# Attention forward and backward with constant matmuls ahead of the gradient bursts, the backward stream two half-steps later, value tiles double buffered, and the normalisation in two parts

## The chip, the cores and the metric

The kernel runs on one core of a Trainium2 chip. The metric is the device time of one execution in microseconds (us), the median over several. The core has five engines that run side by side: TensorE (PE in the profile; its weight loads are listed apart, as PEld), VectorE (DVE), ScalarE (ACT), GpSimd (POOL) and SyncE (SP), whose queue issues nearly all DMAs here. [...]

## The reference

The program computes a layer and its gradients. The layer mixes an attention block and a state-space convolution with a gate. Only the attention part matters for the change:

```python
B, S, D, H = 1, 2048, 576, 32          # Dh = D // H = 18
def _A_ref(x, wqkv, wo):
    qkv = (x @ wqkv).reshape(B, S, 3, H, Dh).transpose(2, 0, 3, 1, 4)
    q, k, v = qkv[0], qkv[1], qkv[2]
    scores = jnp.einsum("bhqd,bhkd->bhqk", q, k) * (Dh ** -0.5)
    p = softmax(scores, axis=-1)
    o = jnp.einsum("bhqk,bhkd->bhqd", p, v)
    return o.transpose(0, 2, 1, 3).reshape(B, S, D) @ wo
...
g = sigmoid((x * gate_w).sum(-1, keepdims=True))
return g * a + (1 - g) * b             # a: attention, b: the convolution
```

The kernel returns this output and the gradients of all twelve differentiated inputs for a given `grad_out`. For attention that means dQ, dK and dV, with P recomputed where it is needed: dV = P^T dO, dP = dO V^T, dS = P * (dP - rowsum(dO * O)), dQ = dS K, dK = dS^T Q.

## The kernel before

The program has stages one after the other: projections and preparation, attention (forward and backward), a stage that forms the weight gradients of attention, the convolution with its gradients, and the sum. The change touches attention alone.

**Tiles.** 32 heads of width 18 are padded to 32 partitions, so four heads fill 128. A head group `g` (8 of them) has transposed tiles `QaT`, `KaT`, `VaT` (128 x 2048) and token-major tiles `Vtok`, `Ktok`, `Qtok`, loaded in `load_group` (L364 on). `QaT`, `KaT` and `Vtok` have two buffers, `VaT`, `Ktok` and `Qtok` one. A unit is a group and one of four blocks of 512 queries: 32 units.

**Two streams in one loop.** The loop over `G` counts half-steps, 32 per unit (`NST`), 1024 in all. In each, the forward stream of one unit computes two score tiles P1 (keys on partitions; two of the four heads), and the backward stream of an earlier unit, `OFF = NST + 5 = 37` half-steps behind (`G2 = G - OFF`), computes two score tiles P3 (queries on partitions) and two tiles P2 = V dO^T. These are the rows: six matmuls of 32 x 128 weights on 512 columns, in two sets of three (x = 0, 1). Each set works on three different 32-row strips of PE, so its three run side by side. P1 and P3 go to PSUM tag `S` (four buffers), P2 to `dP` (two).

**After the rows come the bursts, then ACT and DVE.** The order on PE, ACT, DVE and POOL is the program's own (`manual_schedule`); SP's order is set by the framework. In each half-step, PE runs the rows and then one or two bursts of 128-row, 32-column matmuls, four of which work side by side on the four column strips:

- `G % 4 == 1`: `dv_burst`, 8 matmuls of 512 columns (`accV`), eight tiles `eb` times `dOa`;
- `G % 4 == 2`: `dq_burst`, 8 of 512 columns (`accQ`), two tiles `ds` times `Ktok`;
- `G % 4 == 3` and `0`: half of dK each, 8 of 256 columns (`accK`, from the transposed `dsT`), and after it `accO`, 4 of 512 columns, the forward P V of one key tile.

All three gradient accumulators share one PSUM buffer, `accB`. ACT then takes exp of the P1 tiles (`PT`, L593) and the P3 tiles (`eb`, L597), four in all; DVE multiplies the two P2 tiles by P (`ds`, L602) and then adds the burst's accumulator to its sum in SBUF (`dvacc` L462, `dqa` L479, `dkacc` L503). When a `ds` tile is complete, SP issues its transpose `dsT` (L608).

**At the end of a unit's forward** `post_forward` makes three steps. f0 (ACT) copies `accO` to `oT`. f1, two half-steps later and ahead of that half-step's rows, transposes it on PE into a tile of tag `S` (`ps_o`), and on DVE divides by the row sum (`rl`, `Ob`), scales dO (`dOa`), and forms the row sums of dO * O (`prod`, `dl`, into `dOa`); then SP stores `Ob` to `O_d` (L409). f2, at the same place, has SP transpose `dOa` to `dOaT` (L413), which the backward stream's P2 reads. `dOa` has three buffers by hand.

**Gradients leave** through `store_grad`: an ACT copy `gb` (L419), a DMA transpose `gT` (L421), a POOL copy `dtk` (L423) and a store (L424); once per unit for dQ, eight times per group for dV and dK.

Every matmul is issued by the helper in L30, so the profile shows that line for all of them; they are told apart by their tiles. In `out<-in,in` the streamed operand stands first and the weights second: `ps_P<-QaT_g,KaT_g` is P1, `ps_P<-KaT_g,QaT_g` P3, `ps_P<-dOaT,VaT_g` P2.

## Time and profile before

| | us |
|---|---|
| median of 4 executions | 3944.19 (3938.09 to 3949.21) |
| the profiled execution | 3926.11 |
| its span | 3924.4 |
| first P1 row to last accK result (attention) | 243.1 to 2525.9 |
| PE idle for VaT_g, 392 to 2350 us | 33.0 (7 times) |
| DVE `ds` (L602) idle for PE, same stretch | 202.6 |
| mean granted TensorE clock, whole span | 0.64 of full speed |

The page gives, for each engine, its busy time, and then the span in 40 slices of 98 us, with a digit for the busy share in tenths. The line `PEclk` is the share of full speed that the chip grants TensorE in that slice. Matmuls are pipelined and their ends are modelled, so a PE that reads as busy need not be at its peak rate. A group line has the program line, engine, operation, tiles, shapes and count, then busy time and mean duration of one, then the engine's idle time just before, and what ended it.

### The profile page before, as it was taken

The page shows a single profiled execution, that of the slowest core. Times are in us where ns is not written, and L with a number is a line of the kernel's source. Part 1 is how long each engine was busy: PE and PEld are TensorE (multiplying, and loading weights), DVE is VectorE, ACT ScalarE, POOL GpSimd, SP SyncE. Part 2 cuts the span into 40 slices and gives each one's busy share as a digit, 9 for nine tenths or more (in the row PEclk, how much of TensorE's full clock was granted, in tenths as well). Part 3 has the DMA queues.
Part 4 walks back from the last instruction along what each step waited for, and adds up shares of the span by engine and source line. Part 5 has one row for each costly group of instructions (what it writes and reads, how often), then busy time and mean ns, then how long its engine had stood idle before and what let it go on. Part 6 is the DMA issues. An engine that isn't in the chain of part 4 may idle for free. (4 is left out here: it accounts for less than half of the span.)

```text
span 3924.4 us, 64060 instructions
## 1 busy us (share of the span) xinstructions
PE 3017.0 (77%) x24020; PEld 1067.3 (27%) x24020; DVE 2945.2 (75%) x5131; ACT 2842.0 (72%) x5253; POOL 63.2 (2%) x147
## 2 busy tenths in 40 slices
PE   7979999999999999999999999679344554445421
PEld 2312222222222222222222222145133333333320
DVE  5618878878878878878878878625288888888867
ACT  4559999999999999999989999410266666666610
POOL 0000000000000000000000000100000000000000
PEclk9956666656665656665666667589555555555555
DMA  8535686775686785686776686875455666555456
GB/s 196 170 93 131 135 159 135 137 162 129 134 162 130 136 162 131 138 160 132 143 159 131 138 152 128 193 207 148 71 97 108 110 110 113 104 101 103 85 146 194
DMA packets 1860137, 536.78 MB, mean 137 GB/s; under 512 B 1774991, under 2 KB 1838553, under 8 KB 1859826
## 3 DMA queue, kind: packets, MB, share of 16 engines
q1 hardware_dynamic: 1859826, 532.69, 64.9%
q8 instruction: 189, 3.10, 0.3%
q14 instruction: 122, 1.00, 0.1%
HBM read 99.74 MB, written 60.96 MB: 41 GB/s over the span
## 5 line engine op out<-in xcount | busy, mean ns | idle before, releaser
L602 DVE TENSOR_TENSOR ds<-ps_P,PT 128x512 bf16<-128x512 f32 x2048 | 1359.4, 687 | 351.0 <-PE ps_P L30 225.6
L593 ACT ACTIVATE PT<-ps_P 128x512 bf16<-128x512 f32 x2048 | 1316.1, 647 | 135.9 <-PE ps_P L30 127.1
L597 ACT ACTIVATE eb<-ps_P 128x512 bf16<-128x512 f32 x2048 | 1333.2, 653 | 20.9 <-PE ps_P L30 20.8
L30 PE MATMUL ps_P<-dOaT,VaT_g 32*128 32x512 bf16 x2048 | 1045.6, 537 | 45.6 <-DMA VaT_g<-VaT_d 33.0
L30 PE MATMUL ps_P<-KaT_g,QaT_g 32*128 32x512 bf16 x2048 | 1007.1, 528 | 37.7 <-ACT PT L593 3.2
L30 PE MATMUL ps_P<-QaT_g,KaT_g 32*128 32x512 bf16 x2048 | 960.7, 543 | 34.4 <-DMA KaT_g<-KaT_d 6.0
L30 PEld LDWEIGHTS <-KaT_g 32*128 32x128 bf16 x2048 | 148.5, 101 | 656.6 <-issue 641.6
L30 PEld LDWEIGHTS <-VaT_g 32*128 32x128 bf16 x2048 | 191.8, 96 | 412.9 <-issue 368.2
L30 PE MATMUL accO<-PT,Vtok_g 128*32 128x512 bf16 x2048 | 301.8, 573 | 0.0
L30 PE MATMUL accK<-dsT,Qtok_g 128*32 128x256 bf16 x4096 | 287.5, 374 | 5.5 <-DVE dqa L479 3.5
L30 PE MATMUL accQ<-ds,Ktok_g 128*32 128x512 bf16 x2048 | 238.4, 558 | 1.4 <-DVE dvacc L462 0.8
L30 PE MATMUL accV<-eb,dOa 128*32 128x512 bf16 x2048 | 233.3, 547 | 0.6 <-DVE dkacc L503 0.6
L30 PEld LDWEIGHTS <-QaT_g 32*128 32x128 bf16 x2048 | 172.0, 97 | 187.3 <-issue 175.9
L30 PE MATMUL uvp<-RX,E1e 128*128 128x64 bf16 x1152 | 134.2, 290 | 106.8 <-DVE E1e L901 106.8
L30 PE MATMUL tps<-RX,T0w 128*128 128x32 bf16 x576 | 38.4, 233 | 215.0 <-DVE yd L1036 202.6
L882 ACT ACTIVATE kk<-ph,magc 128x512 f32<-128x512 f32 x144 | 91.0, 685 | 147.5 <-DVE E1e L900 112.7
L30 PE MATMUL ph<-thr,lrow 3*128 3x512 bf16 x288 | 126.2, 567 | 88.0 <-ACT ab L875 60.2
L462 DVE TENSOR_TENSOR dvacc<-dvacc,accV 128x512 f32<-128x512 f32 x224 | 153.3, 684 | 28.8 <-PE accV L30 25.4
L479 DVE TENSOR_TENSOR dqa<-dqa,accQ 128x512 f32<-128x512 f32 x224 | 153.1, 684 | 24.8 <-PE accQ L30 20.5
L30 PEld LDWEIGHTS <-E1e 128*128 128x128 bf16 x1152 | 125.3, 124 | 127.8 <-DVE E1e L901 127.2
L30 PE MATMUL ybp<-Rw,E1n 128*128 128x31 bf16 x1152 | 70.2, 233 | 103.7 <-ACT ydi L973 101.0
L887 DVE SCALAR_TENSOR_TENSOR kk<-kk,ph 128x512 f32<-128x512 f32 x144 | 95.1, 682 | 71.8 <-ACT kk L882 71.7
(267 smaller groups left out, 3329.3 us busy)
## 6 DMA issues: line engine op xcount, KB each, us to landing
T0w<-Kp_d SPq DMA_DIRECT2D x36, 512.0 KB
dsT<-ds SPq DMA_TRANSPOSE x512
dqkv_d<-dtk SPq DMA_DIRECT2D x96, 72.0 KB
dqkv_tok<-dqkv_d SPq DMA_DIRECT2D x1, 6912.0 KB
Md_d<-mst SPq DMA_DIRECT2D x144, 36.0 KB
ga_d<-ga_st SPq DMA_DIRECT2D x16, 288.0 KB
dxm_d<-dxm SPq DMA_DIRECT2D x16, 288.0 KB
skw<-Md_d SPq DMA_DIRECT2D x72, 64.0 KB
```

Of the source, the lines that this page charges most:

```text
L30: return nc.tensor.matmul(out, lhsT=lhsT, rhs=rhs, start=start, stop=stop, **kw)
L462: nc.vector.tensor_tensor(a_, a_, acc, op=A.add)
L479: nc.vector.tensor_tensor(U["dqa"], U["dqa"], acc, op=A.add)
L593: nc.scalar.activation(U["PT"][i][:, j, :], ps, ACT.Exp)
L597: nc.scalar.activation(e, ps, ACT.Exp)
L602: nc.vector.tensor_tensor(U["ds"][i][:, j, :], ps, U["PT"][i][:, j, :], op=A.mult)
L882: nc.scalar.activation(B_["kk"][h][:, 4 * q:4 * q + 4, :], ph, ACT.Identity, bias=magc, scale=1.0)
L887: nc.vector.scalar_tensor_tensor(v_, v_, MAGIC, B_["ph"].pop((h, q)), op0=A.subtract, op1=A.subtract)
```

## The change

Seven things change, all inside the attention stage:

- `fill` issues matmuls of a constant (`J_bf`, a reversed identity, as weights; `ident_bf`, read four times over, as 512 streamed columns) over the whole 128 x 128 array, into the accumulator that the next burst will overwrite. There is one ahead of the dV burst, one ahead of dQ, three ahead of the first half of dK (`NFILL = (1, 1, 3)`).
- `OFF` is `NST + 7` in place of `NST + 5`. The bursts now go by `G2 % 4` and stay at their places within the backward stream; `accO` stays at `G % 4 == 3` and `0` and is now issued ahead of the fill and the burst. So per four half-steps: `accO`, fill, `accV` | `accO`, fill, `accQ` | three fills, `accK` | `accK`.
- `VaT` has two buffers in place of one.
- f1 keeps the transposes, `rl`, `Ob` and `dOa`. f2 takes `prod`, `dl`, the last write to `dOa`, the store to `O_d` and the transpose `dOaT`, and runs one half-step after f1.
- `PT` has 21 buffers in place of 20, `eb` 10 in place of 12, `dOa` two in place of three.
- `oT`, `rl`, `Ob`, `dl` and `dqa` have one buffer in place of two.
- The accumulator of a burst is taken ahead of it and handed over by a list, `ACC`.

```diff
+            NFILL = (1, 1, 3)
...
-                ptp = ctx.enter_context(tc.tile_pool(name="ptp", bufs=20))
+                ptp = ctx.enter_context(tc.tile_pool(name="ptp", bufs=21))
...
-                for u in range(3):
+                for u in range(2):
...
-                    for nm, src, nb in (("QaT", QaT_d[g], 2), ("KaT", KaT_d[g], 2), ("VaT", VaT_d[g], 1)):
+                    for nm, src, nb in (("QaT", QaT_d[g], 2), ("KaT", KaT_d[g], 2), ("VaT", VaT_d[g], 2)):
...
+                        st["Ob"] = Ob
                         nc.vector.tensor_tensor(Ob, po[:, :, :, 0:DH], rlb, op=A.mult)
                         nc.vector.tensor_tensor(da[:, :, :, 0:DH], U["dO"], rlb, op=A.mult)
+
+                    def f2():
+                        da, Ob = U["dOa"], st["Ob"]
                         prod = work.tile([P, TPQ, 4, DH], F32, tag="prod", bufs=1, name="prod")
                         nc.vector.tensor_tensor(prod, da[:, :, :, 0:DH], Ob, op=A.mult)
...
                         nc.sync.dma_start(O_d[:, b * TPQ:(b + 1) * TPQ, 4 * g * DH:4 * (g + 1) * DH], Ob.rearrange("p t a b -> p t (a b)"))
-
-                    def f2():
                         U["dOaT"] = work.tile([P, TPQ, P], BF, tag="dOaT", name="dOaT")
...
-                OFF = NST + 5
+                OFF = NST + 7
...
+                ACC = []
+                fill_r = ident_bf.unsqueeze(1).to_broadcast([P, 4, P])
+
+                def fill(acc, n, w=4):
+                    o_ = acc[:, (4 - w) * P:4 * P].rearrange("p (a b) -> p a b", b=P)
+                    for _ in range(n):
+                        mm(o_, lhsT=J_bf, rhs=fill_r[:, 0:w, :])
+
                 def dv_burst(g, b, kq, half):
                     U = UN[(g, b)]
-                    acc = accB("accV")
+                    acc = ACC.pop()
...
+                    ph = G2 % 4 if 4 <= G2 < NTOT + 4 + (0, 1, 6, 0)[G2 % 4] else None
+                    if ph == 2 and G2 < 10:
+                        ph = None
...
-                                at(("pre", G + 2), f2)
+                                at(("pre", G + 3), f2)
+                    if ph in (0, 1, 2):
+                        ACC.append(accB(("accV", "accQ", "accK")[ph]))
+                        fill(ACC[0], NFILL[ph])
+                    if G2 % 4 == 0 and G2 >= 4:
...
+                            evs.append(dv_burst(g, b, q_ // 2, q_ % 2))
...
+                    if G2 % 4 == 1 and G2 >= 5:
...
+                            evs.append(dq_burst(g, b, q_))
...
+                    if G2 % 4 in (2, 3) and G2 >= 10:
...
+                            e_ = dk_half(g, b, q_, h_, dkst)
...
-                            e = work.tile([P, KB], BF, tag="eb", bufs=12, name="eb")
+                            e = work.tile([P, KB], BF, tag="eb", bufs=10, name="eb")
```

## The prediction

> **What bounds the kernel now.** I read the page first, then the groups of the attention stretch, then its timeline and clock. From the page:

> ```profile
> PE 3017.0 (77%) x24020; PEld 1067.3 (27%) x24020; DVE 2945.2 (75%) x5131; ACT 2842.0 (72%) x5253; POOL 63.2 (2%) x147
> ...
> PE   7979999999999999999999999679344554445421
> ...
> ACT  4559999999999999999989999410266666666610
> ...
> PEclk9956666656665656665666667589555555555555
> ```

> Slices 4 to 25 are the attention part. PE and ACT both read 9, and the TensorE clock is granted at only 0.5 to 0.7. The groups of 392 to 2350 us, by line, operation, shapes and count, busy time, mean ns, idle before:

> ```profile
> L602 DVE TENSOR_TENSOR ds<-ps_P,PT 128x512 bf16<-128x512 f32 x1774 | 1177.7, 687 | 317.2 <-PE ps_P L30 202.6 <-issue 43.9 <-ACT eb L597 41.7
> L597 ACT ACTIVATE eb<-ps_P 128x512 bf16<-128x512 f32 x1774 | 1159.8, 654 | 0.0
> L593 ACT ACTIVATE PT<-ps_P 128x512 bf16<-128x512 f32 x1773 | 1146.4, 647 | 124.2 <-PE ps_P L30 115.5
> L30 PE MATMUL ps_P<-dOaT,VaT_g 32*128 32x512 bf16 x1773 | 912.8, 538 | 40.8 <-DMA VaT_g<-VaT_d 33.0 <-DVE ds L602 5.5 <-DMA dOaT<-dOa 2.0
> ```

> DVE and ACT wait for PE, and PE waits 33.0 us (7 times) for the value tile of a new head group. Then the timeline of one half-step at full clock (start, duration, engine, line, operation):

> ```profile
> 1509.08 0.39 PE L30 MATMUL ps_P<-QaT_g,KaT_g 32*128 32x512 bf16 x1
> ...
> 1510.18 0.38 PE L30 MATMUL ps_P<-dOaT,VaT_g 32*128 32x512 bf16 x1
> 1510.49 0.40 PE L30 MATMUL accK<-dsT,Qtok_g 128*32 128x256 bf16 x8
> 1510.72 0.39 PE L30 MATMUL accO<-PT,Vtok_g 128*32 128x512 bf16 x4
> 1511.04 0.38 PE L30 MATMUL ps_P<-QaT_g,KaT_g 32*128 32x512 bf16 x1
> ```

> From one first row to the next 1.96 us pass. In that time ACT runs four exponentials, whose ends lie 0.49 apart (1511.59, 1512.07, 1512.57), so 4 x 0.49 = 1.96: at full clock ACT is the bound. Measured over the whole stretch (starts of the first P1 row of each half-step, 985 of them with both streams, 284.7 to 2451.5 us) the mean is 2.198. Half-steps 14 to 31 of a unit, away from the unit change, average 2.098; of these the ones wholly at half clock 2.155, wholly at full clock 1.971. Last, the clock in windows (busy us of PE, weight load, DVE, ACT, POOL; then the clock):

> ```profile
> 1504.00:1507.41 3.41, 3.41 (x29) 0.71 (x27) 2.81 (x5) 3.17 (x7) 0.00 (x0) 0.50 0.49 102
> 1507.41:1510.83 3.42, 3.08 (x36) 1.03 (x32) 3.33 (x7) 3.42 (x8) 0.00 (x0) 1.00 0.42 96
> 1510.83:1514.24 3.41, 2.97 (x32) 0.99 (x24) 2.83 (x5) 3.41 (x9) 0.00 (x0) 1.00 0.65 147
> 1514.24:1517.65 3.41, 3.41 (x27) 0.64 (x26) 2.58 (x5) 3.27 (x8) 0.00 (x0) 0.50 0.68 154
> ```

> The clock changes only at steps of 3.41 us. What decides it is not PE's busy time but the share of the array in use. I counted, per window, the columns streamed times the share of the array that the shape occupies (a 32x512 row: 128; the eight of accV or accQ: 1024; eight of accK: 512; four of accO: 512). Of 460 half-clock windows 85 were followed by full clock; their count has a 10th percentile of 2908 and a median of 3072, while 90% of the others lie under 2950. Of 172 full-clock windows 84 were followed by half clock, all with a count under 3190; of the 88 that stayed, 11 lie below 3072. So about 3072 per window is the mark. Four half-steps now hold 24 rows, accV, accQ, 2 accK, 2 accO = 7168; at 7.84 us that is 3120 per window, just at the mark, and full clock is lost after two windows as a rule (27% of windows).

> **The change, part by part.** *Fill.* Five matmuls of 512 columns on the whole array per four half-steps add 2560: 9728 per period. Their price. A 512-column step takes 0.22 us at full and 0.42 at half clock (eight accQ took 0.61 and 1.04, one 0.39 and 0.62). Going from rows to a burst takes 0.31 from start to start at full clock, so 0.09 beside the step, and 0.53 at half; from burst to rows 0.31 and 0.56. Switching to and from a whole-array matmul inside a burst has no row; it lies between 0 (accK to accO, same shape, no gap) and 0.14 (burst to rows at half clock), and I take 0.09. The bursts also move: accO now precedes accV (one half-step) and accQ (the next), then accK alone with three fills, then accK alone. What these read (PT, eb, ds, dsT) is older than the rows ahead of them, so the order adds no wait.

> At full clock, accO + fill + accV: rows to accO 0.31, to fill 0.31, to accV 0.31, second group 0.22, to the next rows 0.31 = 1.46. From the fourth exponential's end to its row 0.06, row 0.39, exponential 0.60: 0.06 + 1.46 + 0.39 + 0.60 = 2.51, where ACT wants 1.96 + 0.49 = 2.45. So two of four half-steps are 0.06 late: 2.02. With accK and three fills 0.31 + 0.44 + 0.31 + 0.11 + 0.21 = 1.38, on time: 1.96, as is the last. Period 7.96, mean 1.99. At half clock 0.41 (first to second rows) + 0.53 + 0.56 + 0.53 + 0.42 + 0.56 = 3.01 for the three filled ones, about 2.1 for the fourth (today's accK median): mean 2.78.

> The count per full window is then 9728 x 3.41 / 7.96 = 4170 on average. But a window over the unfilled half-step holds 16 rows' worth (its own and the next, 1536), one accK (512) and some 0.4 us of burst: about 2880. Sliding a window over this timeline, 11% of positions lie under 3072. The window after such a one starts at a filled burst, dense enough to come back (2816 per 3.01 us = 3190 per window). So I take nine full windows to one half: 30.7 / 1.99 + 3.41 / 3.01 = 16.56 half-steps in 34.1 us = 2.06. Gain (2.098 - 2.06) x 985 = 37 us.

> *Value tiles double buffered.* The load leaves the group change; 33.0 us of PE idle go, up to 34.5 by the seven long half-steps (7.26 mean against 2.33 for others there). Next late there would be Ktok and Qtok, still single: PE's loads wait 2.4 us for Qtok now. Gain 31, bounds 0 to 34.

> *Normalisation in two parts.* Half-steps 1 to 4 of a unit cost 0.91 + 0.38 + 0.57 - 0.24 = 1.6 us over 2.098. Its DVE chain (0.26 + 0.46 + 0.45 + 0.46 + 0.45 + 0.20 = 2.28) stood in one piece ahead of two products of 0.69; now 1.17 and 1.11 in successive half-steps. The second part carries the O_d store and the dOaT transpose to the next half-step on SP's queue, where dsT transposes follow them; with the backward stream two later, dOaT has four half-steps instead of three. The transposes on PE and the wait for rl and Ob before ps_o's buffer comes free remain. I take 0.5 of the 1.6, x 31 units = 16, bounds 0 and 50.

> *Copies on ACT.* With ACT the bound, oT, one gb of dqa and on average two of dvacc and dkacc per unit cost 4 x 0.49 = 1.96; 0.55 of it shows already (half-step 10), about 0.9 falls into the 0.06 gaps. Loss 0.5 x 31 = 16, bounds 0 and 40.

> *Two half-steps later.* Two more with P1 alone (1.12) and with the gradients alone (2.0), two fewer of 2.2: loss 2. Fewer buffers for eb, dOa, dqa, oT: each is read out a half-step or more before its reuse (eb's burst ends some 0.8 us ahead), so nothing; were that cover gone, one wait of that order per period.

> Sum: -37 - 31 - 16 + 16 + 2 = -66. The profiled execution took 3926.1 (span 3924.4), so 3860; it lies 18 under the median 3944.19, so the median becomes **3878**.

> [...]

> **The rivals.**

> *Full clock throughout.* If the count never falls under the mark, the mean is 1.99: (1.99 - 2.098) x 985 = -106, sum -135, **3809**. For it: the average is a third above the mark. Against: the unfilled half-step.

> *Half clock too often (slower).* At half clock a filled half-step costs 3.01 against 2.155 before. The point from which this decides is where the full-clock share of time falls under 0.77: there 1 / (0.77/1.99 + 0.23/2.78) = 2.13, which eats the other terms (-29 / 985 = -0.03). At 0.65 the mean is 2.21: +110 - 29, **4025**. For it: the low window comes round every eight or nine, and the stall at each unit change can drop the clock once more, and a half-clock window over the unfilled half-step holds about 1280 + 1.3/3.0 x 2816 = 2500, below the mark. Against: three dense half-steps in a row.

> *A wait takes the place.* All bursts share one accB buffer, and a fill writes it, so it waits for DVE's evacuation earlier than the burst did; rows and exponentials queue behind it. accQ's last result comes 0.31 x 3 + 0.22 + 0.39 = 1.54 after the rows, the evacuation ends at 2.23, the next fill is due at 2.33: 0.1 to spare, with DVE at 2 x 0.66 + 0.69 = 2.01 of 2.02. Were two fills per period 0.13 late, 246 x 0.26 = 64 would be lost: **3942**, no change.

> *The fill does not count.* If constant operands do not move the clock, its share stays 0.27: 1 / (0.27/1.99 + 0.73/2.78) = 2.51, +406 - 29: **4321**. Nothing in the trace of before shows a matmul on such data.

> **How the numbers follow.** Chances: forecast 0.47, full clock 0.17, the wait 0.13 (0.04 faster, 0.07 same, 0.02 slower), half clock 0.20, not counted 0.03. About 0.2%, 8 us, is what a measurement of this kernel can tell. So faster 0.68, same 0.07, slower 0.25. The forecast's own range is 3836 to 3936: the unseen switch at 0 gives 30 less, at 0.2 some 50 more, and the bounds of the split and copies add to it. The range from full clock to most of the half-clock case is 3805 to 4000; about 0.07 lies below and 0.12 above.

> **What would show it.** Granted clock of 0.9 or more in slices 5 to 24, PE's wait for VaT_g gone, half-steps of 2.02, 2.02, 1.96, 1.96 in full windows and about 3.0 in half ones, the 317 us that ds waits for PE smaller. A clock near 0.8 with PE at 9 means the second rival; idle of PE before the fill, released by dqa or dvacc, the third; 0.6 the fourth. The prediction is wrong if the full-clock share leaves 0.8 to 1, or if the switch to the whole array costs far from 0.09.

## The result, and the profile after

| | before | after |
|---|---|---|
| median, us | 3941.86 (48 runs) | 3950.68 (29 runs) |
| ratio to before | | 1.0027, 95% interval [1.0019, 1.0036] |
| span of the profiled execution, us | 3924.4 | 3950.0 |
| half-step with both streams, mean, us | 2.198 (986 of them) | 2.210 (984) |
| mean granted TensorE clock, 600 to 2300 us | 0.63 | 0.91 |

The change makes the kernel 0.27% slower, where 1.7% faster was forecast. The clock rose, though not quite as far as foreseen (nine full windows to one half would be a mean of 0.95), and the half-steps did not get shorter. The page of the changed kernel, the lines that answer to those of before:

```profile
PE 3031.7 (77%) x25300; PEld 1099.4 (28%) x25300; DVE 2906.2 (74%) x5131; ACT 2841.6 (72%) x5253; POOL 63.0 (2%) x146
...
PE   7979999999989999999999999768345544445421
...
ACT  4549999989989989999989999500266666666610
...
PEclk9958999988989989989989989888655555555555
```

PE has 1280 more matmuls (the fills), the clock line reads 8 or 9 through the attention slices instead of 5 to 7, and ACT falls from 9 to 8 in every third slice or so. The groups of 392 to 2350 us (busy time, mean ns, idle before):

```profile
L619 DVE TENSOR_TENSOR ds<-ps_P,PT 128x512 bf16<-128x512 f32 x1765 | 1153.6, 685 | 180.9 <-PE ps_P L30 179.6 <-issue 0.2
L614 ACT ACTIVATE eb<-ps_P 128x512 bf16<-128x512 f32 x1766 | 1116.6, 632 | 0.0
L610 ACT ACTIVATE PT<-ps_P 128x512 bf16<-128x512 f32 x1765 | 1104.6, 626 | 129.6 <-PE ps_P L30 124.0
L30 PE MATMUL ps_P<-dOaT,VaT_g 32*128 32x512 bf16 x1764 | 698.9, 414 | 1.5 <-DMA dOaT<-dOa 0.7 <-DVE ds L619 0.4
L30 PE MATMUL accK<-ident_bf,J_bf 128*128 128x512 bf16 x663 | 188.8, 395 | 19.1 <-DVE dqa L490 14.3 <-DVE dqa L488 3.4
```

A row now takes 0.41 us on average where it took 0.54, and the wait for VaT_g (33.0 us) is gone. But in the same 1958 us the kernel gets through 1765 tiles where it got through 1774. ACT sits idle for 129.6 us before `PT` (124.0 of them for PE), much as before (124.2, 115.5 for PE). The clock in windows of 3.41 us shows the main reason (window, length, busy us of PE, weight load, DVE, ACT, POOL; then clock, DMA share, GB/s):

```profile
1235.06:1238.47 3.41, 3.41 (x24) 0.72 (x27) 2.16 (x4) 3.19 (x8) 0.04 (x1) 0.50 0.87 168
1238.47:1241.88 3.41, 3.08 (x37) 0.90 (x31) 2.36 (x4) 2.99 (x7) 0.39 (x1) 1.00 0.80 151
1241.88:1245.30 3.42, 3.20 (x31) 0.82 (x24) 2.64 (x6) 3.42 (x8) 0.00 (x0) 1.00 0.61 114
1245.30:1248.71 3.41, 3.41 (x36) 1.01 (x31) 3.34 (x6) 3.38 (x8) 0.00 (x0) 1.00 0.53 100
1248.71:1252.12 3.41, 3.19 (x33) 0.88 (x25) 2.67 (x6) 3.41 (x8) 0.00 (x0) 1.00 0.78 136
1252.12:1255.54 3.42, 3.42 (x24) 0.57 (x20) 2.27 (x4) 2.52 (x6) 0.00 (x0) 0.50 0.75 142
...
1269.19:1272.60 3.41, 3.41 (x24) 0.59 (x20) 2.18 (x4) 2.44 (x6) 0.00 (x0) 0.50 0.80 152
```

In this stretch every fifth window is at half clock, and in it ACT is idle for 0.2 to 1 us. The window ahead of the second one, 1248.71 to 1252.12, on PE:

```profile
1249.79 0.40 PE L30 MATMUL accK<-dsT,Qtok_g 128*32 128x256 bf16 x8
1250.12 0.39 PE L30 MATMUL ps_P<-QaT_g,KaT_g 32*128 32x512 bf16 x1
...
1251.46 0.39 PE L30 MATMUL ps_P<-dOaT,VaT_g 32*128 32x512 bf16 x1
1251.77 0.40 PE L30 MATMUL accO<-PT,Vtok_g 128*32 128x512 bf16 x4
1252.10 0.61 PE L30 MATMUL accV<-ident_bf,J_bf 128*128 128x512 bf16 x1
1252.64 1.04 PE L30 MATMUL accV<-eb,dOa 128*32 128x512 bf16 x8
```

It is the window over the half-step without a fill: but for the tail of the burst before, the accK half at 1249.79 is its only gradient burst, and the next fill starts as it ends. Counted as in the prediction it holds 2850 columns, under the mark of about 3072 that the trace of before gave. Of 78 such drops from 300 to 2400 us, 48 come after a window that begins in the half-step with three fills, mostly late in it, and 26 after one that begins in the half-step with none; 30 of them lie exactly five windows after the one before, 10 lie ten windows after. 62 of the drops last one window, the other 16 two to eight.

### The profile page after: what moved, and what is told of

It reads as the page before. It is cut to its first block, busy times and chain, and to the rows that moved or that the text cites. A ratio compares the mean times of both kernels' runs of the same rounds, so it can differ in the third digit from the quotient of the medians.

```text
span 3950.0 us, 66344 instructions
## 1 busy us (share of the span) xinstructions
PE 3031.7 (77%) x25300; PEld 1099.4 (28%) x25300; DVE 2906.2 (74%) x5131; ACT 2841.6 (72%) x5253; POOL 63.0 (2%) x146
## 5 line engine op out<-in xcount | busy, mean ns | idle before, releaser
L610 ACT ACTIVATE PT<-ps_P 128x512 bf16<-128x512 f32 x2048 | 1270.8, 625 | 142.1 <-PE ps_P L30 135.8
L614 ACT ACTIVATE eb<-ps_P 128x512 bf16<-128x512 f32 x2048 | 1285.7, 630 | 24.7 <-PE ps_P L30 24.6
L30 PE MATMUL ps_P<-dOaT,VaT_g 32*128 32x512 bf16 x2048 | 807.2, 413 | 5.1 <-DVE ds L619 3.5
L30 PE MATMUL ps_P<-KaT_g,QaT_g 32*128 32x512 bf16 x2048 | 736.8, 406 | 45.2 <-ACT PT L610 11.1
L30 PE MATMUL ps_P<-QaT_g,KaT_g 32*128 32x512 bf16 x2048 | 724.3, 415 | 44.2 <-ACT PT L610 13.1
L30 PEld LDWEIGHTS <-VaT_g 32*128 32x128 bf16 x2048 | 174.9, 92 | 375.4 <-issue 370.6
L30 PEld LDWEIGHTS <-KaT_g 32*128 32x128 bf16 x2048 | 138.1, 94 | 398.7 <-issue 395.2
L30 PE MATMUL accK<-ident_bf,J_bf 128*128 128x512 bf16 x768 | 217.8, 394 | 24.6 <-DVE dqa L490 18.2
L30 PE MATMUL accO<-PT,Vtok_g 128*32 128x512 bf16 x2048 | 235.3, 444 | 0.0
L30 PEld LDWEIGHTS <-J_bf 128*128 128x128 bf16 x1344 | 120.5, 99 | 363.0 <-issue 294.8
L30 PE MATMUL accK<-dsT,Qtok_g 128*32 128x256 bf16 x4096 | 211.1, 284 | 6.8 <-DMA Qtok_g<-QaT_d 6.7
L30 PE MATMUL uvp<-RX,E1e 128*128 128x64 bf16 x1152 | 134.2, 290 | 106.6 <-DVE E1e L918 106.6
L30 PE MATMUL tps<-RX,T0w 128*128 128x32 bf16 x576 | 38.4, 233 | 215.0 <-DVE yd L1053 190.9
L30 PE MATMUL ph<-thr,lrow 3*128 3x512 bf16 x288 | 128.0, 580 | 86.9 <-ACT ab L892 59.3
L30 PE MATMUL accV<-eb,dOa 128*32 128x512 bf16 x2048 | 191.2, 457 | 0.0
L30 PEld LDWEIGHTS <-QaT_g 32*128 32x128 bf16 x2048 | 153.1, 92 | 135.4 <-issue 132.0
L30 PE MATMUL accQ<-ds,Ktok_g 128*32 128x512 bf16 x2048 | 171.6, 415 | 4.8 <-DMA Ktok_g<-KaT_d 4.8
L30 PEld LDWEIGHTS <-E1e 128*128 128x128 bf16 x1152 | 125.2, 123 | 127.3 <-DVE E1e L918 126.7
```

The lines of the kernel that those rows point to most:

```text
L30: return nc.tensor.matmul(out, lhsT=lhsT, rhs=rhs, start=start, stop=stop, **kw)
L610: nc.scalar.activation(U["PT"][i][:, j, :], ps, ACT.Exp)
L614: nc.scalar.activation(e, ps, ACT.Exp)
```

## The experiments

Times are medians; ratios are of means, to the kernel before on the same chip (its median there 3936 to 3944), with 95% intervals. "Full period" is the sum, over the four places in a period, of the median half-step that lies wholly at full clock, each from its first P1 row to the next one's. A "drop" is a change from full to half clock; drops and half-clock windows are counted from 300 to 2400 us. Eleven kernels ran.

**Without the fills.**

```diff
-            NFILL = (1, 1, 3)
+            NFILL = (0, 0, 0)
```

> The changed kernel with its five fills per period left out (NFILL 0, 0, 0); all else stays. Theory A (the clock eats the gain: the fills raise the share of full clock, but the one half-step without a fill drops it every fourth or fifth window, and a filled period costs 11.3 us at half clock against 8.0): without fills the granted clock in attention falls from 0.90 to 0.60-0.68, a period at full clock 7.84 us, at half clock 8.8-9.2, and the time is within 25 us of the changed kernel (3930 to 3975). Rival B (the fills cost by themselves, through PE time and the single accB buffer, also at full clock): 40 us or more faster than the changed kernel, below 3910. Rival C (bunching accO with accV and accQ is what costs): still slower than the kernel before, 3960 or more, with dV and dQ half-steps of about 2.4 us at half clock.

3972.6, ratio 1.0076 [1.0059, 1.0093]. The clock of 600 to 2300 us, in the changed kernel and then without fills:

```profile
600.00:2300.00 1700.00, 1609.57 (x13340) 434.13 (x13336) 1329.65 (x2256) 1585.24 (x3166) 30.92 (x72) 0.91 0.80 142
600.00:2300.00 1700.00, 1594.50 (x12242) 401.09 (x12246) 1336.63 (x2231) 1564.76 (x3129) 29.47 (x69) 0.71 0.80 141
```

PE is busy 94% of the time without fills at a clock of 0.71, and 95% in the changed kernel at 0.91: the constant matmuls do move the clock, and busy time does not tell it. They bring 0.5%. That falls on theory A's side and against B as a whole, with the clock a little above A's bound. But C fits as well, by its time and by its half-steps: at half clock the one with accO and accQ takes 2.37 us, the one with accO and accV 3.00.

**Bursts spread again, no fills.** accO goes to the two accK half-steps.

```diff
-                    if G % 4 in (3, 0) and G >= 3:
-                        i_ = (G - 3) // 4 * 2 + (1 if G % 4 == 0 else 0)
+                    if G % 4 in (1, 2) and G >= 2:
+                        i_ = (G - 2) // 4 * 2 + (1 if G % 4 == 1 else 0)
```

> As e1, and accO moved two half-steps, so that it stands with the two accK halves as in the kernel before: the stall edits alone (double-buffered value tiles, split normalisation, stream two later) with bursts spread as before. Theory A: half-steps 16 to 31 of a unit as in the kernel before (2.09 us), granted clock 0.6-0.65, the stalls at the unit change 2 us per unit less: 45 to 70 us faster than the kernel before, 3875 to 3900. Rival (the stall edits bring nothing because something else is late at the unit change): within 15 us of the kernel before.

3920.8, ratio 0.9951 [0.9936, 0.9966]: 19 us faster than before, less than expected, and 1.25% faster than e1. So C is right in part: having accO beside accV and accQ costs 49 us without fills (a period at half clock takes 9.21 us in e1 and 8.65 here). PE's waits show what the stall edits ran into (total, times, longest):

```profile
PEld L30 <- DMA Qtok_g<-QaT_d: 27.8, 7, 5.1
PE accK L30 <- DMA Qtok_g<-QaT_d: 24.9, 7, 4.8
```

The wait for VaT_g at the seven group changes, in half-step 5 of a unit, became one for Qtok_g in half-step 17.

**Bursts spread, with fills.** accO as in e2, with one fill ahead of accV, accQ and the first accK half (`NFILL` 1, 1, 1); then two at the last place (1, 1, 2).

> As e2 with one fill ahead of accV, accQ and the first accK half. Counted on a full-clock timeline of 1.96 us per half-step, the emptiest window holds 3072 columns, and 1% of positions are under the mark. Theory A: granted clock 0.95 or more in attention, half-steps 16 to 31 of 1.97 to 2.0 us, time 3770 to 3830. Rival B (the fill's own cost or the accB wait): full clock, but half-steps of 2.1 or more, time above 3880.

> As e3_bal_fill111 with two fills ahead of the first accK half. Theory A: the same as with one within 15 us, since the emptiest window is the one over the half-step without a fill (3072 columns in both). Rival B: slower by 20 us or more, about 245 x 0.1 to 0.2.

With one: 3867.7, ratio 0.9804 [0.9783, 0.9824], clock 0.94, full period 7.84 us, which is ACT's 16 x 0.49. The period held and the size did not (3770 to 3830 was expected): half-steps 16 to 31 average 2.08, Qtok_g is waited for here too (24.9 us, all in half-step 17), and the clock drops 41 times. Runs of 46 to 60 windows at full clock occur between them. With two: 3903.9, ratio 0.9895 [0.9878, 0.9912], full period 7.98. Here rival B was right: a second fill in that half-step lies on the path, 0.14 us a period.

**Value tile back to one buffer; normalisation back to one part.** Each alone, in the changed kernel.

```diff
-                    for nm, src, nb in (("QaT", QaT_d[g], 2), ("KaT", KaT_d[g], 2), ("VaT", VaT_d[g], 2)):
+                    for nm, src, nb in (("QaT", QaT_d[g], 2), ("KaT", KaT_d[g], 2), ("VaT", VaT_d[g], 1)):
```

> The changed kernel with VaT back in one buffer; all else stays. Theory A (the double buffer took the 33 us wait away, but Qtok and Ktok, still single, are late next and give a part back: 11.5 us in the changed kernel's trace): PE's wait for VaT_g returns with 25 to 35 us, that for Qtok_g and Ktok_g goes to under 4, time 10 to 25 us above the changed kernel, 3960 to 3976. Rival (the next late load takes all of it): within 8 us of the changed kernel.

3966.7, ratio 1.0088 [1.0056, 1.0120]. The wait for VaT_g is back, and that for Qtok_g falls to 2.1:

```profile
PE ps_P L30 <- DMA VaT_g<-VaT_d: 40.0, 7, 6.9
```

The second buffer is worth 0.6%, 24 us (by the intervals some 13 either way), as theory A had it.

```diff
-                        st["Ob"] = Ob
...
-                    def f2():
-                        da, Ob = U["dOa"], st["Ob"]
...
+                    def f2():
                         U["dOaT"] = work.tile([P, TPQ, P], BF, tag="dOaT", name="dOaT")
...
-                                at(("pre", G + 3), f2)
+                                at(("pre", G + 2), f2)
```

> The changed kernel with the normalisation in one part again (prod, dl and the O_d store in f1, the dOaT transpose at the same place); all else stays. The prediction priced the split at 16 us (0 to 50): by it 3960 to 3975. Rival (the wait for ps_o and the ACT copies set the stall at the unit change, not the length of DVE's chain): within 8 us of the changed kernel.

3980.1, ratio 1.0125 [1.0085, 1.0165]: the split is worth about 1.0%, 39 us (some 16 either way), over twice the 16 of the prediction. Half-step 3 of a unit goes from 2.47 to 3.89 us, and PE's rows wait for the `dP` buffer that DVE has not emptied:

```profile
PE ps_P L30 <- DVE ds L617: 24.7, 29, 0.9
```

In the changed kernel this wait is 0.4 us.

**A fourth fill ahead of the first accK half.**

```diff
-            NFILL = (1, 1, 3)
+            NFILL = (1, 1, 4)
```

> The changed kernel with four fills in place of three ahead of the first accK half: more work for PE. On the full-clock timeline the emptiest window then holds 3175 columns, over the mark of about 3072 (2879 with three), and the accK half-step gets 0.1 to 0.15 us late, so a period at full clock takes 8.1 us. Theory A: the drops every fifth window go, granted clock in attention 0.95 or more against 0.905, time 20 to 60 us below the changed kernel (3890 to 3930). Rival B (the fills cost more than they bring): 20 us or more above it, 3970 or more.

3985.4, ratio 1.0136 [1.0101, 1.0171]. Theory A fell here, and the time is rival B's. The clock rose only to 0.93, the drops fell from 78 to 67, and the full period went from 7.98 to 8.22, twice what was expected: 0.24 us for one fill of 0.22. The half-step had no slack left, and the timeline that I slid the window over was no longer the real one.

**Every second accO moved, nothing else.** Same instructions, same five fills; the accO of even key tiles goes one half-step earlier, into the half-step without a fill.

```diff
-                    if G % 4 in (3, 0) and G >= 3:
-                        i_ = (G - 3) // 4 * 2 + (1 if G % 4 == 0 else 0)
+                    if G % 2 == 0 and G >= 2:
+                        i_ = G // 2 - 1
```

> The changed kernel with the same instructions and the same five fills, but the accO of every even key tile is issued one half-step earlier, in the half-step that has no fill (G % 4 == 2 in place of 3). On the full-clock timeline the emptiest window rises from 2879 to 3072 columns and the positions under 3072 fall from 11% to 1%. Theory A (the half-step without a fill drops the clock): the drops every fifth window go, granted clock in attention 0.93 or more, period at full clock 7.9 us, time 3880 to 3915. Rival B (what is lost is the fills' own cost at full clock, and the order does not matter): within 15 us of the changed kernel, 3935 to 3965.

3898.7, ratio 0.9880 [0.9861, 0.9898]: 1.5%, 58 us, below the changed kernel. Its full period is 7.98 us, the same. What differs is the clock:

```profile
600.00:2300.00 1700.00, 1581.59 (x13690) 464.85 (x13691) 1367.33 (x2315) 1614.02 (x3246) 31.18 (x73) 0.95 0.81 146
```

There are 28 drops instead of 78, and 53 half-clock windows instead of 116. Rival B is out: with the same work and the same length at full clock, where the work stands costs 58 us. PE's waits do not explain them: the one for Qtok_g rises from 6.7 to 17.4 us, and the one for DVE to empty accQ's result falls from 19.1 to 8.3.

```profile
PE accK L30 <- DMA Qtok_g<-QaT_d: 17.4, 7, 3.3
```

**The next late load.** Qtok in four tiles, one per query block (same memory, same bytes), so that a block's buffer comes free units ahead of the group change; in the changed kernel and in the spread one with fills 1, 1, 1. And another way to the same end: fills 1, 1, 1 with OFF = NST + 5, which spreads the bursts as before, PT 20 buffers, Qtok in two.

```diff
-                    for nm, src, nb in (("Vtok", VaT_d[g], 2), ("Ktok", KaT_d[g], 1), ("Qtok", QaT_d[g], 1)):
+                    for nm, src, nb in (("Vtok", VaT_d[g], 2), ("Ktok", KaT_d[g], 1)):
...
+                    T["Qtok"] = []
+                    for c_ in range(NQ):
+                        q_ = ga.tile([P, TPQ, 4, HP], BF, tag=f"Qtok{c_}", bufs=1, name="Qtok_g")
+                        nc.sync.dma_start_transpose(out=q_.rearrange("p t h w -> p t (h w)"), in_=QaT_d[g][:, c_ * KB:(c_ + 1) * KB])
+                        T["Qtok"].append(q_)
...
- ... lhsT=grp_t[g]["Qtok"][:, b * TPQ + qb, j, :],
+ ... lhsT=grp_t[g]["Qtok"][b][:, qb, j, :],
```

> The changed kernel with Qtok as four tiles, one per query block, each loaded by a transpose of its own; same bytes, same memory. A block's tile comes free when its unit's backward ends, long before the group change. Theory A (part of what the value tiles gained went into the next late load): PE's wait for Qtok_g goes to 1 us or less, Ktok_g stays with 5 to 10, time 5 to 20 us below the changed kernel, 3930 to 3945. Rival (the stall at the group change only moves on, to Ktok_g or dOaT): within 5 us.

> The spread bursts with fills 1, 1, 1 (e3_bal_fill111, ratio 0.980) and Qtok as four tiles. Theory A: the 25 us that PE waits for Qtok_g there go, and the clock drops that follow them; half-steps 16 to 31 of 2.0 us, time 3825 to 3850, ratio 0.970 to 0.976. Rival (Ktok_g takes its place): ratio 0.978 or more, with Ktok_g in PE's waits.

> Spread bursts as in the kernel before (OFF = NST + 5, accO with the accK halves, PT 20 buffers), fills 1, 1, 1, split normalisation, VaT double buffered, and Qtok in two buffers too. Theory A: against e3_bal_fill111 (3868) the 25 us that PE waits for Qtok_g go, half-steps 16 to 31 come to 2.0 us or less, time 3835 to 3860. Rival (another late transfer, Ktok_g or dOaT, which has one half-step less here, takes its place): within 10 us of 3868 or slower, with that transfer named in PE's waits.

In the changed kernel: 3933.6, ratio 0.9963 [0.9947, 0.9978], 25 us less (some 7 either way; 5 to 20 was expected), though PE's own wait for Qtok_g was only 6.7 us; the drops fall from 78 to 71 with it, and the half-clock windows from 116 to 96. In the spread one: **3835.7, ratio 0.9716 [0.9696, 0.9736]**, the fastest of all, 2.8% below the kernel before; clock 0.95, half-steps 16 to 31 of 2.01. The third way: 3895.7, ratio 0.9901 [0.9872, 0.9931], a miss, as its rival said. Qtok_g is no longer waited for, but with the backward stream only two half-steps behind f2 the transposed dOa is, at every unit:

```profile
PE ps_P L30 <- DMA dOaT<-dOa: 50.0, 30, 3.0
```

## Why the prediction was wrong, point by point

- **Full clock: the sum is right, its parts are not.** Predicted 7.96 us a period, measured 7.98. But the two half-steps after accV and accQ were to be 0.06 late each; between the last exponentials of successive half-steps lie 2.10 us after accV, 1.96 after accQ, 1.99 after the three fills and 1.96 after the last accK half (medians at full clock). That the sum fits so well is partly luck. The unseen switch to a whole-array matmul, taken as 0.09 beside the step (0.31 from start to start), took 0.32 from accO to fill and from fill to accV, 0.54 at half clock.
- **Half clock: right for the period.** Predicted 3.01 for a filled half-step, 2.1 for the last and 2.78 on average; measured medians 3.84, 3.03, 2.91 and 1.51 (8 to 19 half-steps each), on average 11.29 / 4 = 2.82. (They run from first P1 row to first P1 row, and split a period unevenly at full clock too: 2.83, 1.96, 1.98, 1.21.)
The 11% of positions under the mark came out too: sliding a window over the changed kernel's stretches at full clock gives 13%.
- **"So I take nine full windows to one half": the step that failed.** It was to follow from the 11%, as if windows fell anywhere, and from a single half-clock window per drop. Measured (300 to 2470 us): 119 of 633 windows at half clock, 79 drops, so 6.5 full windows to 1.5 half. Put into the prediction's own formula: 6.5 x 3.41 / 1.99 + 1.5 x 3.41 / 3.01 = 12.84 half-steps in 27.3 us = 2.125, against 2.06. So the clock term is (2.125 - 2.098) x 985 = +27 and not -37; with the other terms as forecast the sum is -2, the median 3942. That is 64 us of the 73 that were missed, and e9 gets 58 us back by moving every second accO into the emptiest window. Either ratio alone would give 2.08 or 2.09, so each has about half of it.
- *Why 6.5.* All 247 changes of the clock in the changed kernel's trace lie on one grid of 3.413 us, and the loop falls into step with it for a while. Eight half-steps without a half-clock window take 16.01 us, with exactly one 17.26 (medians of 37 and 57 cases), so a drop costs 1.25 us, where the prediction's rates make it 1.15. Five windows are 17.07: after a drop nearly the same position comes back, about 0.2 us earlier each time, until it has left the low places. Of 77 distances between drops 30 are exactly five windows, where chance at 13% per window would give about 7 (an estimate: 77 x 0.87^3 x 0.13).
- *Why 1.5.* Of the 38 half-clock windows beyond the first of a drop, 27 lie in drops that begin in half-steps 10 to 19 of the units in which the backward stream takes up a new group. There PE waits for Ktok_g (half-step 12) and Qtok_g (17):

```profile
PE accK L30 <- DMA Qtok_g<-QaT_d: 6.7, 5, 2.9
PE accQ L30 <- DMA Ktok_g<-KaT_d: 4.8, 6, 1.3
```

- **What the formula leaves open.** Half-steps 14 to 31, to which the 2.06 belongs, in fact average 2.174, not 2.125. The prediction takes this mean for all 985 half-steps, which makes it 48 us more; PE's wait for Qtok_g explains 6.7 of them, and the cause of the rest stays open. On the other side, half-steps 0 to 13 together cost 99 us above that mean before and 35 now, a gain of 64 where the value tiles, the normalisation and the copies were to bring 31. The two misses partly cancel, so it is partly luck that 3942 comes so near the measured time.
- **accO beside accV and accQ, a part of "the bursts also move": not priced by itself.** What it reads is old enough, as said, but it leaves one half-step nearly empty and three heavy. From e1 and e2 it costs 49 us without fills. The whole change then reads as a chain of ratios: stall edits and later stream 0.9951, accO bunched 1.0076, fills 1.0027; that is -19, +49 and -19 us.
- **Value tiles: the wait went, and the next one was priced too low.** Predicted 31, measured 24. I named Ktok and Qtok as next late, but priced them from the 2.4 us of before. They hold 11.5 us of PE idle in the changed kernel, Qtok 24.9 in e2, and Qtok alone is worth 25 us in e10. There 20 half-clock windows go with the 6.7 us of wait; that the clock is the rest of those 25 us is argued, not tested apart.
- **Normalisation: right in sign, mis-sized.** 16 predicted (0 to 50), about 39 measured.
- **The accB wait** of the third rival is there: the first of the three fills waits 76 times in 300 to 2400 us for DVE to empty accQ's result, 19.1 us in all. It was not tested by itself; e8, and e3 with two fills against one, show that each further fill in the first accK half-step lies on the path.
- **"The fill does not count" is out**: e1 against the changed kernel, 0.71 to 0.91, with PE busy alike in both, 94% and 95%.
- The copies on ACT and the two half-steps at both ends were not tested alone.

The outcome lies between the forecast and the second rival, whose mechanism it is. The full-clock share is 0.81, above the 0.77 at which that rival was to decide, and inside the 0.8 to 1 outside which the prediction was to count as wrong. Both limits were too low: the 0.77 was worked out with the 2.78 of a whole period at half clock, but the half-clock windows lie over filled half-steps, and with their 3.01 it becomes 0.81.

## What to carry to other kernels

If the clock goes with the work per fixed window, as it did here in windows of 3.41 us, count the emptiest window, not the average, and spread work to raise it before adding any: every second accO moved by a half-step was worth more (58 us) than five fills a period (19 us). A loop whose periods, with the delay of one drop, add up to nearly a whole number of windows comes back to the same position, so a share of positions is not by itself the share of windows. When a late transfer is removed, look up which single-buffered one has the fewest half-steps between its last use and its next first use; here Qtok had three, and splitting it by the order of use cost no memory.
